# A layer out with the weights stationary and 384 tokens moving, its sums kept with outputs on partitions

## The chip, the core and the metric

The kernel runs on one core of a Trainium2 chip. The metric is the device time of one execution in microseconds (us), the median over several runs. The engines are named as in the profile: PE is the matrix engine (its weight loads stand apart as PEld), DVE is VectorE, ACT is ScalarE, POOL is GpSimd, and SP is the queue that issues nearly all DMAs. Each runs its own instructions in the order in which the program gives them.

## What is computed

Attention within chunks of 64 tokens, then a mixture of four experts with given shares (the first part), then a gated layer (the second part), in float32:

```python
attn = softmax(scale * q_c @ k_c.T); x = attn @ v_c        # (4, 8, 576, 64), 36 * 64 tokens a head
x = x.transpose(0, 2, 1, 3).reshape(2304, 512)
p = domain_probs / (domain_probs.sum(-1, keepdims=True) + 1e-09)
for e in range(4):
    out += p[:, e:e + 1] * (np.maximum(x @ w1[e], 0) @ w2[e])   # w1[e]: 512 x 1024, w2[e]: 1024 x 512
g = out @ w_gate; result = (g * sigmoid(g) * (out @ w_val)) @ w_out  # 1536 wide
```

## The kernel before, in words

The 2304 tokens go in three passes of 768 (six blocks of 128, or two halves of 384, `TT`). Part one runs over the passes, and in each over 16 sets of 256 hidden units, `sets`; two sets make a group (eight groups a pass, 24 in all, two groups to an expert). Part two does the same over the gated layer.

**Layer in** (`product`, lines 628 to 648; `half_k`, 618): a set's layer in is a 2x2 block product that is made of seven products, six matmuls each, weights stationary and 384 tokens moving. Each number is held as a rounded high part and a low part, and hi*hi, hi*lo and lo*hi are summed, three matmuls a term. The products' sums are put together by DVE (`plus`, 612) and kept by ACT (`keep`, 608). `done` (554) makes of a sum the hidden tile of a set: ACT writes the high part `hh` (559), DVE the low part `hl` (560), both [128 hidden units, 384 tokens].

**Layer out of part one** (`layer2`, 664 to 681): for each block of 128 tokens, four pieces of 128 hidden units with three matmuls each: the hidden tile's 128 tokens are stationary, 512 outputs of `w2` move, so a tile `y` in PSUM has tokens on partitions and is full after 12 matmuls. `gather` (751 to 764) multiplies it by the token's share `prob` of this expert, one number a partition, and adds it to the block's sum `acc`, in one DVE operation (762; 760 for the first group of a pass). After the last group of a pass `turn_x1` (768 to 777) turns each block's sum with four PE transposes, ACT copies it back, and SP stores it, since the next layer needs features on partitions.

**The order** is written out by hand (`order`, 1013 to 1020, and the loop from 1037). After every four and every three products there is a gap, in which the layer out of the group before gets its share of matmuls from the generator `two`: 18 where a group has two sets (1055), 12 for the first group (1044), 9 in each of the four steps `ahead` before the loop (993). `later` (162) puts a piece of work off by so many products. Weights for a product are made or loaded six products ahead (`LEAD`, `prepare`, 1026). `run_tasks` (966) lets background work in, among it the conversion of the second part's weights to its operands (`make_ops`, 452).

**Attention** of the first six blocks comes at the beginning, with the first products beside it; that of the other twelve is the list `rest` (953 to 957), whose stages (`att_scores`, `att_turn`, `att_values`, `att_out`: lines 255, 294, 317, 336) are done one at a time, four in the steps `ahead` and then after five of every seven products (1088). Scores are reduced and shifted by DVE (276, 277), exponentiated by ACT (283), turned by PE (287), multiplied with the values by PE (323), divided by DVE (330) and turned back by PE.

**Places in PSUM.** A `y` tile has two banks (`psY`), and two more (`psA`) once attention is through (1093). Until then the attention stages take turns in `psA`.

Of the kernel before, what the change touches and what calls it, by code (L numbers as in the profile page):

```python
# [10 lines left out]
F32 = mybir.dt.float32  # L11
# [80 lines left out]
def attention_moe_gated(  # L92
# [21 lines left out]
    ident = const.tile([P, P], F32, name="ident")  # L114
    prob = const.tile([P, NS, NE], F32, name="prob")

    xs = [dram.tile([2, P, KD, TT], F32, name=f"x_{s}") for s in range(2 * NPASS)]

    xt_d = [dram.tile([4, P, 2, TT], F32, name=f"xt_{s}") for s in range(2 * NPASS)]
    w_d = [dram.tile([NPROD, P, 2, 2 * P], F32, name=f"w_{n}") for n in range(NPAIRS + 2 * NPAIRS2)]  # L120
    w2_d = [dram.tile([P, 2, DM], F32, name=f"w2_{c}") for c in range(4 * NG1)]
# [40 lines left out]
    def later(d, f):  # L162
        deferred.setdefault(now[0] + d, []).append(f)
# [376 lines left out]

    gates = {}
    val, out_op = {}, {}
# [11 lines left out]
    def done(n, c, t, src):  # L554
# [8 lines left out]
        elif m == 0:  # L563
            sg = gates[c, t] = sg_p.tile([P, TT], F32, tag="sg", name=f"sg_{n}_{c}_{t}")

# [98 lines left out]
    def layer2(G):  # L664

        for b in range(BLOCKS):
            pool, tag = y_places[b % len(y_places)]
            y = pool.tile([P, DM], F32, tag=tag, name=f"y_{G}_{b}")
            c = slice(b % HALF * P, (b % HALF + 1) * P)
            for j in range(4):  # L670
                hh, hl = hid[G, j, b // HALF]
                w = w2op[G, j]
                nc.tensor.matmul(y, hh[:, c], w[:, 0], start=(j == 0), stop=False)  # L673
                yield
                nc.tensor.matmul(y, hh[:, c], w[:, 1], start=False, stop=False)  # L675
                yield
                nc.tensor.matmul(y, hl[:, c], w[:, 0], start=False, stop=(j == 3))  # L677
                if j < 3:
                    yield
            gather(G, b, y)  # L680
            yield

# [67 lines left out]

    def gather(G, b, y):
        part, s, g = part_of(G)
        a = s * BLOCKS + b
        if g == 0:
            acc[b] = acc_p.tile([P, DM], F32, tag="acc", name=f"acc{part}_{a}")
        sum_ = acc[b]
        if part == 1:
# [8 lines left out]
    turned = [-9]  # L766

    def turn_x1(s, b, sum_):
        turned[0] = now[0]
        src = sum_.rearrange("p (h k) -> p h k", k=CH)  # L770
        ps = transpose(att_ps(f"x1t_{s}_{b}", (psA, "a")), src).rearrange("p h k -> p (h k)")


        nc.scalar.copy(sum_, ps)
        half, c = divmod(b, HALF)
        d = xs[NPASS + s][half, :, :, c * P : (c + 1) * P]
        later(1, lambda: nc.sync.dma_start(d, sum_.rearrange("p (k t) -> p k t", t=P)))


    with tc.manual_schedule():  # L780
        acc_p = ctx.enter_context(tc.tile_pool(name="acc", bufs=8))
        h_p = ctx.enter_context(tc.tile_pool(name="h", bufs=12))
# [37 lines left out]
        clear(nc.gpsimd, vbd[2])  # L820
        clear(nc.gpsimd, vbd[3])
        nc.gpsimd.dma_start(prob, probs)
        att_load(0)
# [31 lines left out]
        def shares():  # L855

            sm = t_p.tile([P, NS], F32, tag="sum", name="prob_sum", bufs=3)
            nc.vector.tensor_reduce(out=sm, in_=prob, op=ALU.add, axis=AX.X)
            nc.vector.tensor_scalar_add(sm, sm, EPS)
            nc.vector.reciprocal(sm, sm)  # L860
            nc.gpsimd.tensor_tensor(out=prob, in0=prob, in1=sm.unsqueeze(2).to_broadcast(prob.shape), op=ALU.mult)

# [74 lines left out]
        for j in range(HALF):  # L937
            first_split("t2", j)
        tick()
        next_plain()  # L940
# [96 lines left out]
        for o in order:  # L1037
            if o is None:
# [4 lines left out]
                if G == 0:  # L1043
                    for _ in range(12):
                        next(two)
# [14 lines left out]
            if o == (N1, 0):  # L1060
                assert not tasks and not running, (len(tasks), len(running))
                raw64_cm.close()
                sg_p = ctx.enter_context(tc.tile_pool(name="sg", bufs=6, side="right"))
                wow_p = ctx.enter_context(tc.tile_pool(name="wow", bufs=2, side="right"))
# [23 lines left out]
            if rest and now[0] % NPROD < 5:  # L1088
                stage, a = rest.pop(0)
                stage(a, (psA, "a"))  # L1090
                if not rest:
# [30 lines left out]
def _lay_out(q, k, v, moe_domain_probs, moe_w1, moe_w2, moe2_w_gate, moe2_w_val, moe2_w_out):  # L1122
# [22 lines left out]
    def quads64(w):  # L1145
# [8 lines left out]
        "vt": np.ascontiguousarray(vt),  # L1154
        "probs": np.ascontiguousarray(moe_domain_probs.reshape(NS, P, NE).transpose(1, 0, 2)),
        "w1": np.ascontiguousarray(np.concatenate([quads(moe_w1[e]) for e in range(NE)])),
# [19 lines left out]
```

## Time and profile before

| | |
|---|---|
| median of 3 runs | 1246.08 us (1244.86 to 1246.33) |
| the profiled execution | 1245.16 us, its span 1243.3 us |
| PE, PEld busy | 1226.5 us (99%), 1131.5 us (91%) |
| DVE busy | 794.0 us (64%) |
| ACT, POOL busy | 538.7 us (43%), 595.3 us (48%) |
| DMA | 359.94 MB, mean 289 GB/s |

The span goes from the first to the last instruction of the profiled execution; about 2 us lie around it. Engines overlap, so the busy times don't add up. A matmul's duration in the profile is longer than its distance to the next one, since matmuls are pipelined: a run of them is measured from start to start. "Idle before" is the time in which an engine had nothing running ahead of an instruction, and the name behind it is what ended that wait.

### The profile page before, as it was taken

The page shows a single profiled execution, that of the slowest core. Times are in us where ns is not written, and L with a number is a line of the kernel's source. Part 1 is how long each engine was busy: PE and PEld are TensorE (multiplying, and loading weights), DVE is VectorE, ACT ScalarE, POOL GpSimd, SP SyncE. Part 2 cuts the span into 40 slices and gives each one's busy share as a digit, 9 for nine tenths or more (in the row PEclk, how much of TensorE's full clock was granted, in tenths as well). Part 3 has the DMA queues.
Part 4 walks back from the last instruction along what each step waited for, and adds up shares of the span by engine and source line. Part 5 has one row for each costly group of instructions (what it writes and reads, how often), then busy time and mean ns, then how long its engine had stood idle before and what let it go on. Part 6 is the DMA issues. An engine that isn't in the chain of part 4 may idle for free.

```text
span 1243.3 us, 21100 instructions
## 1 busy us (share of the span) xinstructions
PE 1226.5 (99%) x7216; PEld 1131.5 (91%) x7216; DVE 794.0 (64%) x1352; ACT 538.7 (43%) x1192; POOL 595.3 (48%) x611
## 2 busy tenths in 40 slices
PE   7999999999999999999999999999999999999998
PEld 6888888899888999898889889999999999999998
DVE  6766666666636766765566666455667656685576
ACT  4554434345424454544354344334435344344331
POOL 5553434477517776846376867312333222233221
PEclk9999999999999999999999999999999999999999
DMA  9588886799797999897899999866888797788774
GB/s 224 168 273 281 277 271 222 252 323 337 277 354 263 361 325 352 310 380 277 285 368 331 347 395 311 290 226 233 292 322 296 262 312 261 250 312 295 277 234 153
DMA packets 179594, 359.94 MB, mean 289 GB/s; under 512 B 19216, under 2 KB 46352, under 8 KB 179488
## 3 DMA queue, kind: packets, MB, share of 16 engines
q1 hardware_dynamic: 178688, 357.25, 82.6%
q10 hardware_dynamic: 768, 1.31, 0.4%
q8 instruction: 58, 0.95, 0.3%
q14 instruction: 48, 0.39, 0.1%
q0 software_dynamic: 32, 0.04, 0.0%
HBM read 258.90 MB, written 99.61 MB: 288 GB/s over the span
## 4 chain that ended last, share of the span: by engine, by line
PE 81%; DMA 7%; DVE 3%; issue 3%; POOL 2%; ACT 2%; SPq 1%; POOLq 0%; DVEq 0%; ACTq 0%
PE y L673 9%; PE y L677 9%; PE y L675 9%; PE lx L624 8%; PE lx L626 7%; PE lx L625 7%; PE ox L739 5%; PE lz L624 4%; PE oz L739 4%; PE lz L626 4%; PE lz L625 4%; DMA w<-w 3%; PE lw L624 2%; PE lw L626 2%; PE lw L625 2%
## 5 line engine op out<-in xcount | busy, mean ns | idle before, releaser
L673 PE MATMUL y<-w,hh 128*128 128x512 f32 x576 | 228.1, 396 | 0.0
L677 PE MATMUL y<-w,hl 128*128 128x512 f32 x576 | 226.4, 393 | 0.0
L675 PE MATMUL y<-w,hh 128*128 128x512 f32 x576 | 225.6, 392 | 0.2 <-POOL w L126 0.2
L126 POOL TENSOR_TENSOR w<-raw,w 128x256 fp32r<-128x256 f32 (+1 forms) x156 | 143.5, 938 | 149.7 <-ACT w L125 131.9
L126 POOL TENSOR_TENSOR ol<-sg,oh 128x384 fp32r<-128x384 f32 x72 | 80.5, 1129 | 267.1 <-ACT oh L125 225.7
L559 ACT ACTIVATE hh<-sum_p 128x384 fp32r<-128x384 f32 x90 | 47.2, 525 | 221.0 <-DVE sum_p L612 221.0
L762 DVE SCALAR_TENSOR_TENSOR acc<-y,prob,acc 128x512 f32<-128x512 f32 x126 | 91.1, 743 | 65.3 <-PE y L677 65.1
L677 PEld LDWEIGHTS y<-w,hl 128*128 128x128 f32 x576 | 108.0, 188 | 24.1
L673 PEld LDWEIGHTS y<-w,hh 128*128 128x128 f32 x576 | 108.2, 188 | 21.4 <-issue 1.4
L675 PEld LDWEIGHTS y<-w,hh 128*128 128x128 f32 x576 | 108.2, 188 | 21.3 <-POOL w L126 0.7
L612 DVE TENSOR_TENSOR sum_p<-lx,p 128x384 f32<-128x384 f32 x81 | 44.9, 554 | 94.7 <-PE lx L626 93.4
L560 DVE SCALAR_TENSOR_TENSOR hl<-sum_p,hh 128x384 fp32r<-128x384 f32 x90 | 63.0, 700 | 62.4 <-ACT hh L559 62.4
L126 POOL TENSOR_TENSOR w_made<-raw,w_made 128x256 fp32r<-128x256 f32 x84 | 68.3, 822 | 66.3 <-ACT w_made L125 54.3
L125 ACT ACTIVATE w<-raw 128x256 fp32r<-128x256 f32 (+1 forms) x156 | 67.5, 454 | 5.4 <-DVE raw L396 3.2
L125 ACT ACTIVATE oh<-sg 128x384 fp32r<-128x384 f32 x72 | 36.5, 525 | 70.4 <-DVE sg L573 70.0
L608 ACT COPY u<-lx 128x384 f32<-128x384 f32 x81 | 38.6, 477 | 65.0 <-PE lx L626 64.9
L624 PE MATMUL lz<-t1h,w 128*128 128x384 f32 x162 | 55.3, 341 | 1.7 <-DMA w<-w 1.7
L624 PE MATMUL lz<-b22h,w 128*128 128x384 f32 x162 | 55.8, 344 | 1.1 <-ACT p L608 0.9
L624 PE MATMUL lw<-b21h,w 128*128 128x384 f32 x162 | 54.8, 339 | 0.7 <-DMA w<-w 0.7
L125 ACT ACTIVATE o<-sg 128x384 fp32r<-128x384 f32 x54 | 26.5, 520 | 66.8 <-DVE sg L129 66.8
L624 PE MATMUL lx<-t2h,w 128*128 128x384 f32 x162 | 55.0, 340 | 0.3 <-DMA w<-w 0.3
L626 PE MATMUL lx<-t3h,w 128*128 128x384 f32 x162 | 54.9, 339 | 0.0
(270 smaller groups left out, 3421.0 us busy)
## 6 DMA issues: line engine op xcount, KB each, us to landing
w<-w SPq DMA_DIRECT2D x567, 256.0 KB, 5.3
w<-w SPq DMA_DIRECT2D x96, 512.0 KB, 6.0
w<-w_made SPq DMA_DIRECT2D x84, 256.0 KB, 5.7
wo_t<-wo_t SPq DMA_DIRECT2D x36, 512.0 KB, 4.8
wo_b<-wo_b SPq DMA_DIRECT2D x27, 512.0 KB, 4.2
raw<-w SPq DMA_DIRECT2D x19, 512.0 KB, 4.3
raw<-w SPq DMA_DIRECT2D x32, 256.0 KB, 4.3
sums<-x SPq DMA_DIRECT2D x40, 192.0 KB, 5.4
```

Source lines behind the costliest of these rows:

```text
L125: nc.scalar.activation(h, src, AF.Copy)
L126: (lo or nc.vector).tensor_tensor(out=l, in0=src, in1=h.bitcast(F32), op=ALU.subtract)
L559: nc.scalar.activation(h, src, AF.Relu)
L560: nc.vector.scalar_tensor_tensor(out=l, in0=src, scalar=0.0, in1=h.bitcast(F32), op0=ALU.max, op1=ALU.subtract)
L624: nc.tensor.matmul(ps, w[:, 0, c], xh[:, k], start=f, stop=False, skip_group_check=True)
L625: nc.tensor.matmul(ps, w[:, 0, c], xl[:, k], start=False, stop=False, skip_group_check=True)
L626: nc.tensor.matmul(ps, w[:, 1, c], xh[:, k], start=False, stop=e, skip_group_check=True)
L673: nc.tensor.matmul(y, hh[:, c], w[:, 0], start=(j == 0), stop=False)
L675: nc.tensor.matmul(y, hh[:, c], w[:, 1], start=False, stop=False)
L677: nc.tensor.matmul(y, hl[:, c], w[:, 0], start=False, stop=(j == 3))
L739: nc.tensor.matmul(o, left[:, c], w[:, k, right], start=start and t % 2 == 0 and k == 0 and i == 0, stop=k == 1 and i == 2, skip_group_che ...
L762: nc.vector.scalar_tensor_tensor(out=sum_, in0=y, scalar=p, in1=sum_, op0=ALU.mult, op1=ALU.add)
```

## The change

The weights of the layer out become the stationary operand, 128 outputs at a time, and a half's 384 hidden columns move. A `y` tile then has 128 outputs on partitions and 384 tokens along the row, and is full after 12 matmuls as before; there are eight such tiles a group (two halves, four output pieces) in place of six blocks. The share of a token now varies along the row, so a row of 384 shares is loaded for each half and expert, the same on all partitions (`load_share`), from a small tensor in DRAM to which the turned shares are written at the beginning (`shares_turn`). `gather` multiplies the tile by that row and then adds it to the sum, in two operations. The sums already stand with features on partitions, so `turn_x1` and its transposes go, and each sum is stored as it is. A tile buffer of attention goes (`e`, three to two), the stages in `rest` are put into another order, and two of the six places for sigmoid tiles move to another pool. At the beginning two weight splits come ahead of a block's softmax, and a background task starts three products later. Shares are laid out by expert on the host.

```diff
@@ layer2
-        for b in range(BLOCKS):
-            y = pool.tile([P, DM], F32, tag=tag, name=f"y_{G}_{b}")
-            c = slice(b % HALF * P, (b % HALF + 1) * P)
-            for j in range(4):
-                hh, hl = hid[G, j, b // HALF]
-                w = w2op[G, j]
-                nc.tensor.matmul(y, hh[:, c], w[:, 0], start=(j == 0), stop=False)
-                nc.tensor.matmul(y, hh[:, c], w[:, 1], start=False, stop=False)
-                nc.tensor.matmul(y, hl[:, c], w[:, 0], start=False, stop=(j == 3))
-            gather(G, b, y)
+        for half in range(2):
+            for k in range(KD):
+                y = pool.tile([P, DM], F32, tag=tag, name=f"y_{G}_{half}_{k}")[:, :TT]
+                c = slice(k * P, (k + 1) * P)
+                for j in range(4):
+                    hh, hl = hid[G, j, half]
+                    w = w2op[G, j]
+                    nc.tensor.matmul(y, w[:, 0, c], hh, start=(j == 0), stop=False)
+                    nc.tensor.matmul(y, w[:, 1, c], hh, start=False, stop=False)
+                    nc.tensor.matmul(y, w[:, 0, c], hl, start=False, stop=(j == 3))
+                gather(G, half, k, y)
@@ gather, turn_x1
-            p = prob[:, a, g * NE // NG1 : g * NE // NG1 + 1]
-            if g == 0:
-                nc.vector.tensor_scalar(out=sum_, in0=y, scalar1=p, scalar2=None, op0=ALU.mult)
-            else:
-                nc.vector.scalar_tensor_tensor(out=sum_, in0=y, scalar=p, in1=sum_, op0=ALU.mult, op1=ALU.add)
-            if g == NG1 - 1:
-                later(2 + b % 2, lambda: turn_x1(s, b, sum_))
-    def turn_x1(s, b, sum_):
-        ...
+    def load_share(s, e, half):
+        t = share[half] = pb_p.tile([P, TT], F32, tag=f"pb{half}", name=f"share_{s}_{e}_{half}")
+        a = e * NS + s * BLOCKS + half * HALF
+        row = p_d[a : a + HALF].rearrange("a t -> (a t)")
+        nc.sync.dma_start(t, row.unsqueeze(0).to_broadcast([P, TT]))
+        ...
+        nc.vector.tensor_tensor(out=sum_ if g == 0 else y, in0=y, in1=share[half], op=ALU.mult)
+        if g > 0:
+            nc.vector.tensor_tensor(out=sum_, in0=y, in1=sum_, op=ALU.add)
+        if k == KD - 1 and (g + 1) * NE // NG1 != e and (s, e) != (NPASS - 1, NE - 1):
+            later(2, lambda: load_share(*divmod(s * NE + e + 1, NE), half))
+        if g == NG1 - 1:
+            later(2, lambda: nc.sync.dma_start(xs[NPASS + s][half, :, k], sum_))
@@ the beginning
+        def shares_turn():
+            ps = att_ps("shares", where()).rearrange("p h k -> p (h k)")[: NE * NS, :P]
+            nc.tensor.transpose(ps, prob.rearrange("p e a -> p (e a)"), ident)
+            t = t_p.tile([P, P], F32, tag="sum", name="prob_turned", bufs=3)
+            nc.scalar.copy(t[: NE * NS], ps)
+            nc.sync.dma_start(p_d[:], t[: NE * NS])
         att_turn(3, where())
+        w_plain(0, ORDER[:2])
         att_soft(4)
         att_sums(3)
         att_exp(4)
-        w_plain(0, ORDER[:2])
         ...
         att_out(4, where())
+        shares_turn()
         att_values(5, where())
@@ order of attention, shares of the gaps, tasks
-        for a in range(BLOCKS, NS + 2):
-            for stage, b in ((att_scores, a), (att_values, a - 2), (att_turn, a - 1), (att_out, a - 2)):
+        for a in range(BLOCKS, NS + 1):
+            for stage, b in ((att_turn, a - 1), (att_scores, a), (att_values, a - 1), (att_out, a - 1)):
-            for _ in range(9):
+            for _ in range(12):
-                    for _ in range(12):
+                    for _ in range(16):
-                    for _ in range(12 * BLOCKS // (2 * size)):
+                    for _ in range(48 // size):
-            if o == (NPAIRS + 2, 1):
+            if o == (NPAIRS + 2, 4):
-            if not (last_of_pass(n) or last_of_pass(n + 1) and i >= 5 or now[0] - turned[0] < 2):
+            if not (last_of_pass(n) or last_of_pass(n + 1) and i >= 5):
@@ places
-        pool, how = (acc_p, dict(tag="acc")) if a < BLOCKS else (at_p, dict(tag="e", bufs=3))
+        pool, how = (acc_p, dict(tag="acc")) if a < BLOCKS else (at_p, dict(tag="e", bufs=2))
-            sg = gates[c, t] = sg_p.tile([P, TT], F32, tag="sg", name=f"sg_{n}_{c}_{t}")
+            pool, tag = (sg_p, "sg") if sg_count[0] % 6 < 4 else (raw2_p, "raw2")
+            sg_count[0] += 1
+            sg = gates[c, t] = pool.tile([P, TT], F32, tag=tag, name=f"sg_{n}_{c}_{t}")
```

## Rows read from the trace of the kernel before

**Rows 1.** The page, part 1: busy us, share of the span, instructions of each engine
```profile
PE 1226.5 (99%) x7216; PEld 1131.5 (91%) x7216; DVE 794.0 (64%) x1352; ACT 538.7 (43%) x1192; POOL 595.3 (48%) x611
```
**Rows 2.** Waits of PE, longest in total first: us, times, longest us
```profile
PE plz L624 <- ACT w L125: 2.3, 2, 1.9
```
**Rows 3.** Groups of DVE by form: count, busy us, mean ns of one, idle before
```profile
L762 DVE SCALAR_TENSOR_TENSOR acc<-y,prob,acc 128x512 f32<-128x512 f32 x126 | 91.1, 743 | 65.3 <-PE y L677 65.1
L560 DVE SCALAR_TENSOR_TENSOR hl<-sum_p,hh 128x384 fp32r<-128x384 f32 x90 | 63.0, 700 | 62.4 <-ACT hh L559 62.4
...
L612 DVE TENSOR_TENSOR sum_p<-lx,p 128x384 f32<-128x384 f32 x81 | 44.9, 554 | 94.7 <-PE lx L626 93.4 <-ACT raw L440 1.3
```
**Rows 4.** Waits of DVE from 450 to 500 us
```profile
DVE sum_p L612 <- PE lx L626: 5.1, 3, 1.8
DVE acc L762 <- PE y L677: 1.6, 1, 1.6
```
**Rows 5.** Waits of DVE from 500 to 550 us
```profile
DVE sum_p L612 <- PE lx L626: 2.3, 2, 1.7
```
**Rows 6.** Timeline of PE from 503 us: start us, duration us, instruction
```profile
504.07 0.39 PE L673 MATMUL y<-w,hh 128*128 128x512 f32 x1
...
508.24 0.34 PE L624 MATMUL lx<-t3h,w 128*128 128x384 f32 x1
...
512.43 0.39 PE L673 MATMUL y<-w,hh 128*128 128x512 f32 x1
...
519.72 0.39 PE L673 MATMUL y<-w,hh 128*128 128x512 f32 x1
```
**Rows 7.** Timeline of PE from 334 us, at a turn of a sum
```profile
334.59 0.60 PE L287 MATMUL x1t<-ident,acc 128*128 128x128 f32 x4
334.95 0.42 PE L624 MATMUL lz<-b22h,w 128*128 128x384 f32 x1
335.21 0.34 PE L625 MATMUL lz<-b22l,w 128*128 128x384 f32 x1
```
**Rows 8.** Timeline from 130 us: a block's values, their division, the next stage
```profile
131.92 1.09 PE L323 MATMUL av<-vbd,et 128*64 128x128 f32 x16
...
134.11 0.60 PE L287 MATMUL et<-ident,e 128*128 128x128 f32 x4
...
134.79 0.68 DVE L330 TENSOR_TENSOR e<-av,rs 128x512 f32<-128x512 f32 x1
```
**Rows 9.** Timeline from 55 us: raw sums, the first rest block's scores, its exponential
```profile
56.24 1.35 DVE L396 TENSOR_TENSOR raw<-raw 128x256 f32<-128x256 f32 x2
...
57.22 1.09 PE L261 MATMUL s<-kbd,q 128*64 128x128 f32 x16
...
59.81 0.63 ACT L283 ACTIVATE e<-e 128x512 f32<-128x512 f32 x1 [3.77 <-DVE e L277]
```
**Rows 10.** Timeline from 312 us: start of a group's layer out
```profile
312.37 0.39 PE L673 MATMUL y<-w,hh 128*128 128x512 f32 x1
...
314.41 0.54 DVE L560 SCALAR_TENSOR_TENSOR hl<-lx,hh 128x384 fp32r<-128x384 f32 x1
...
315.07 0.50 PE L675 MATMUL y<-w,hh 128*128 128x512 f32 x1 [0.22 <-POOL w L126]
```
**Rows 11.** Timeline from 535 us: start of a later group's layer out
```profile
535.56 0.39 PE L673 MATMUL y<-w,hh 128*128 128x512 f32 x1
...
537.28 0.54 DVE L560 SCALAR_TENSOR_TENSOR hl<-lx,hh 128x384 fp32r<-128x384 f32 x1
```
**Rows 12.** Timeline from 21 us
```profile
24.63 0.44 PE L624 MATMUL plz<-b11h,w 128*128 128x384 f32 x1 [1.91 <-ACT w L125]
```
**Rows 13.** Timeline from 34 us
```profile
35.65 1.09 PE L323 MATMUL av<-vbd,et 128*64 128x128 f32 x16
35.66 0.32 POOL L861 TENSOR_TENSOR prob<-prob,prob_sum 128x72 f32<-128x72 f32 x1
```
**Rows 14.** DMA issues: size, median us from issue to landing
```profile
sums<-x SPq DMA_DIRECT2D x40, 192.0 KB, 5.4
```

More of the change, by code (lines that the diff above doesn't have):

```diff
@@ L114, in attention_moe_gated @@
     ident = const.tile([P, P], F32, name="ident")
-    prob = const.tile([P, NS, NE], F32, name="prob")
     xs = [dram.tile([2, P, KD, TT], F32, name=f"x_{s}") for s in range(2 * NPASS)]
     xt_d = [dram.tile([4, P, 2, TT], F32, name=f"xt_{s}") for s in range(2 * NPASS)]
+    p_d = dram.tile([NE * NS, P], F32, name="p")
     w_d = [dram.tile([NPROD, P, 2, 2 * P], F32, name=f"w_{n}") for n in range(NPAIRS + 2 * NPAIRS2)]
@@ L539, in hidden_tiles @@
         return h, l
-    gates = {}
+    gates, sg_count = {}, [0]
     val, out_op = {}, {}
@@ L664, in layer2 @@
     def layer2(G):
[L666 to L681 removed]
+        for half in range(2):
+            for k in range(KD):
+                pool, tag = y_places[(half * KD + k) % len(y_places)]
+                y = pool.tile([P, DM], F32, tag=tag, name=f"y_{G}_{half}_{k}")[:, :TT]
[4 more added lines that the diff above has]
+                    nc.tensor.matmul(y, w[:, 0, c], hh, start=(j == 0), stop=False)
+                    yield
+                    nc.tensor.matmul(y, w[:, 1, c], hh, start=False, stop=False)
+                    yield
+                    nc.tensor.matmul(y, w[:, 0, c], hl, start=False, stop=(j == 3))
+                    if j < 3:
+                        yield
+                gather(G, half, k, y)
+                yield
     def layer_out(G):
@@ L749, in layer_out, with gather @@
                         yield
-    def gather(G, b, y):
-        part, s, g = part_of(G)
-        a = s * BLOCKS + b
-        if g == 0:
-            acc[b] = acc_p.tile([P, DM], F32, tag="acc", name=f"acc{part}_{a}")
-        sum_ = acc[b]
-        if part == 1:
-            p = prob[:, a, g * NE // NG1 : g * NE // NG1 + 1]
-            if g == 0:
-                nc.vector.tensor_scalar(out=sum_, in0=y, scalar1=p, scalar2=None, op0=ALU.mult)
-            else:
-                nc.vector.scalar_tensor_tensor(out=sum_, in0=y, scalar=p, in1=sum_, op0=ALU.mult, op1=ALU.add)
-            if g == NG1 - 1:
-                later(2 + b % 2, lambda: turn_x1(s, b, sum_))
-    turned = [-9]
-    def turn_x1(s, b, sum_):
[L769 to L777, printed above, removed]
+    share = {}
+    def load_share(s, e, half):
[3 more added lines that the diff above has]
+        nc.sync.dma_start(t, row.unsqueeze(0).to_broadcast([P, TT]))
+    def gather(G, half, k, y):
+        _, s, g = part_of(G)
+        e = g * NE // NG1
+        if g == 0:
+            acc[half, k] = acc_p.tile([P, DM], F32, tag="acc", name=f"acc1_{s}_{half}_{k}")[:, :TT]
+        sum_ = acc[half, k]
+        nc.vector.tensor_tensor(out=sum_ if g == 0 else y, in0=y, in1=share[half], op=ALU.mult)
[5 more added lines that the diff above has]
+            later(2, lambda: nc.sync.dma_start(xs[NPASS + s][half, :, k], sum_))
     with tc.manual_schedule():
+        pb_p = ctx.enter_context(tc.tile_pool(name="pb", bufs=1))
         acc_p = ctx.enter_context(tc.tile_pool(name="acc", bufs=8))
@@ L821, in attention_moe_gated @@
         clear(nc.gpsimd, vbd[3])
+        prob = t_p.tile([P, NE, NS], F32, tag="sum", name="prob", bufs=3)
         nc.gpsimd.dma_start(prob, probs)
@@ L857, in shares @@
             sm = t_p.tile([P, NS], F32, tag="sum", name="prob_sum", bufs=3)
-            nc.vector.tensor_reduce(out=sm, in_=prob, op=ALU.add, axis=AX.X)
+            nc.vector.tensor_reduce(out=sm, in_=prob.rearrange("p e a -> p a e"), op=ALU.add, axis=AX.X)
             nc.vector.tensor_scalar_add(sm, sm, EPS)
             nc.vector.reciprocal(sm, sm)
-            nc.gpsimd.tensor_tensor(out=prob, in0=prob, in1=sm.unsqueeze(2).to_broadcast(prob.shape), op=ALU.mult)
+            nc.gpsimd.tensor_tensor(out=prob, in0=prob, in1=sm.unsqueeze(1).to_broadcast(prob.shape), op=ALU.mult)
+        def shares_turn():
[4 more added lines that the diff above has]
+            nc.sync.dma_start(p_d[:], t[: NE * NS])
         def turn(a):
@@ L938, in attention_moe_gated @@
             first_split("t2", j)
+        for half in range(2):
+            load_share(0, 0, half)
         tick()
@@ L1062, in attention_moe_gated @@
                 raw64_cm.close()
-                sg_p = ctx.enter_context(tc.tile_pool(name="sg", bufs=6, side="right"))
+                sg_p = ctx.enter_context(tc.tile_pool(name="sg", bufs=4, side="right"))
                 wow_p = ctx.enter_context(tc.tile_pool(name="wow", bufs=2, side="right"))
@@ L1154, in _lay_out @@
         "vt": np.ascontiguousarray(vt),
-        "probs": np.ascontiguousarray(moe_domain_probs.reshape(NS, P, NE).transpose(1, 0, 2)),
+        "probs": np.ascontiguousarray(moe_domain_probs.reshape(NS, P, NE).transpose(1, 2, 0)),
         "w1": np.ascontiguousarray(np.concatenate([quads(moe_w1[e]) for e in range(NE)])),
```

## The prediction

> **What bounds the kernel now.** I read the busy shares first, then who PE waits for, then where VectorE (DVE) has room. PE is busy for 1226.5 of 1243.3 us [rows 1]; a busy PE alone proves little, so the waits come next: sixteen kinds, the largest 2.3 us, which lies in the first 30 us [rows 2]. So the sum is that of PE's stream: what leaves it is gained in full, and whatever makes PE wait is lost in full. DVE is busy for 64% [rows 1], but its free time isn't all room. It runs its work in order, and after each layer-in sum it stands idle until ScalarE has made the rounded half: 62.4 us before one of the three groups of such halves alone [rows 3]. What it could give away is the idle time that PE ends. That is 5.1 + 1.6 = 6.7 us of 50 at 450 to 500 [rows 4] and 2.3 us of 50 at 500 to 550 [rows 5]. The reader is to see a full PE beside an engine with little slack in just the part of the kernel that the change loads.
>
> **The stream itself.** A group's layer out is 72 matmuls of 512 moving columns before and 96 of 384 after: the same columns, a third more instructions. What 384 columns cost is shown by the layer-in products, which have that shape. In one stretch 18 y matmuls start at 504.07 and the next product at 508.24: 4.17 us. The 24 product matmuls behind them take 508.24 to 512.43: 4.19 us [rows 6]. So a gap's share (18 before, 24 after) costs 0.02 us more; 24 groups have 96 such shares: +1.9 us. Bounds: nothing if the rates are equal per column, and +5 us if each share costs 0.05 us more, some products being slower than these. I take 1.9, the rows being of the same shape and the same moment. The Trainium skill (TensorE: Matmul & The Clock Gate, section Back-to-back issue gap) gives a warm matmul N/2.4 + 2.5 ns; as an estimate from it, 576 more matmuls would cost 1.4 us, half a microsecond less than my term. The same section's sustained figures, 131 ns at 512 columns and 81 at 128, speak against the change: on a line between them 384 columns take 114 ns, and the estimate is 36 us slower. The trace has 232 ns where that page has 131, so here the measurement decides and that rule gets no chance.
>
> **The turned sums.** 18 blocks (six in each of three passes) lose four transposes each. One such turn starts at 334.59, the product behind it at 334.95, and that product's first matmul holds the next one back to 335.21: 0.36 + 0.26 us [rows 7], where a matmul of this shape alone takes 4.19 / 24 = 0.175. 0.36 + 0.26 - 0.18 = 0.44 us each; 18 of them: **-7.9 us**. PE had no idle time there that could have hidden them. ScalarE loses 18 copies of the turned sums; its share isn't on the path, so I count nothing. The six 256 KB stores of a pass become eight of 192 KB with the same bytes.
>
> **VectorE.** A y tile was one operation of 743 ns; it is now a multiplication that writes back into PSUM and an addition. No row shows DVE writing PSUM. The nearest is a 128x384 operation with one operand in PSUM, 554 ns; I have no reason to go lower, and the upper end is 700 ns, the mean of the 128x384 that contends for SBUF [rows 3]. I take 554, so 1.11 us per tile (0.55 in the first group of a pass, which only multiplies). A set of products (15.65 us, 504.07 to 519.72 [rows 6]) has three tiles before and four after: 4 x 1.11 - 3 x 0.74 = +2.2 us of DVE per set. At 450 to 500 there are 6.7 / 50 x 15.65 = 2.1 us of room per set, just enough; at 500 to 550 there are 0.7, too little [rows 4, 5]. So DVE runs late in places, and the question is what PE needs from it soon.
>
> First, the low half of the group's last hidden tile. Its subtraction stands in DVE's queue behind the gap's two tiles, which now take 2.22 instead of 1.49 us: 0.73 us later where DVE is behind already. It is needed by the twelfth y matmul of the next gap, which starts 11 x 0.174 = 1.92 us after the gap's first, not 11 x 0.232 = 2.55. At 312.37 the gap starts, and the subtraction ends at 314.95; 315.68 against 314.29 would be a wait of 1.4, of which 0.4 is there already (the eleventh matmul, which waits for POOL, starts at 315.07, where 312.37 + 10 x 0.232 = 314.69) [rows 10]: +1.0. At 535.56 and 537.82 [rows 11]: 538.55 against 537.48: +1.1. Elsewhere I see more room, though late tiles of the gap before may add as much again. I take +2.1, bounds 0 and +5.
>
> Second, attention, moved in its order. Before, a block's values and its last transposes had another block's turn between them; now there is one product. Where the block falls one product behind a gap, the values start at 131.92, DVE's division (queued behind the rest of the slot) ends at 135.47, and the stage that would now be those transposes starts at 134.11 [rows 8]: PE waits 1.4 us. By the list's order against the five slots of seven this happens to two blocks: +2.8. Three more come one slot later; with a product more, some 1.1 us, in between, 0.3 each: +0.9. The rest have a gap of 4.2 us in between: nothing. Bounds: 0 if the division overtakes nothing but comes sooner, +7 if DVE's added load delays all five by another 0.7.
>
> Third, in the first steps the first rest block is turned one step after its scores, not two. Scores at 57.22, exponential ended at 60.44 [rows 9]. Now the first y tile's multiplication (0.55) stands ahead of the two raw sums (1.35) that had been done by then, so the exponential ends some 0.9 us later, about 61.4, and the y matmuls in between end at about 60.4: +1.0, bounds 0 and 2.
>
> **The beginning.** Two weight splits go ahead of an exponential; the matmul at 24.63 waited 1.91 us for them [rows 12], so up to 1.9 is to be had. The turn of the shares is one transpose, which needs the divided shares; these end at 35.98 where PE would come at 35.65 [rows 13]: a wait of 0.3, and about 0.4 for itself. I take 0 for both, bounds -1.9 and +1.
>
> **Transfers.** 24 rows of shares are loaded, 192 KB each in SBUF; the nearest row of that size lands in 5.4 us [rows 14], and a row is needed two gaps or more after its load: nothing. Its issue on SP's queue waits for DVE's last tile of the half, and the weight loads queue behind it; they are issued six products ahead. The stores that waited there for a turned sum go. If a share row came late, each of 22 would cost up to a few us; I see no reason. The sigmoid tiles still come from six places, so they cost nothing.
>
> **Sum.** -7.9 + 1.9 + 2.1 + 2.8 + 0.9 + 1.0 + 0 = +0.8 us on the profiled execution's 1245.2, so 1246.0. The median of the runs shown is 0.9 us above that execution: **1247 us**. About 0.2%, 2.5 us, is what a measurement here can tell from no change; this is inside.
>
> **Rivals.**
> Faster, because the waits don't come: DVE takes its work earlier in gaps that now have two tiles evenly, and the late operations still have their few hundred ns. Then -7.9 + 1.9 = -6.0, 1240 us. For it: PE waits for DVE almost nowhere now [rows 2]. Against it: the transposes right behind their division [rows 8]. With half of the waits it is 1243.5. Chance 0.27.
> Slower, because DVE becomes the bound in pass two: it decides once a drain costs more than the room. If the addition takes 700 ns [rows 3], a tile takes 1.25 and a set 4 x 1.25 - 2.23 = 2.8 us more; at 500 to 550, 3.2 sets lack 2.1 each, at 450 to 500 0.7 each: 8.9 us, of which 1.1 stands in the sum already: 1247 + 8 = 1255. For it: the little room at 500 to 550 [rows 5]. Against it: the PSUM row of 554 [rows 3]. Chance 0.25.
> Slower through the instruction count: at the +5 bound of the stream, 1250. Chance 0.10.
>
> **Numbers.** The forecast has 0.38, with a range of its own from 1244 to 1249. Faster 0.27, same 0.38, slower 0.35. The range from 1240 to 1256 reaches to both rivals and leaves out the far sides, where all bounds fall together.
>
> **What would show it.** Right: no x1t rows; 24 y matmuls in 4.17 to 4.20 us; DVE busy up by some 90 us; PE rows that wait for "DVE e L330" at two blocks in the first 230 us and for the low half at a few group starts, 4 to 7 us in all. Wrong: PE waits under 2 us (first rival), DVE idle time ended by PE gone over tens of microseconds and PE waits over 12 us (second), y runs over 4.22 us (third), or waits of PE or DVE on a share row.

## The result and the profile after

The kernel after takes 1263.7 us (median of 6 runs, 1259.75 to 1267.34), the kernel before 1246.2 us beside it: a ratio of 1.0137 [1.0116, 1.0159], 17.5 us slower. The prediction was 1247 us with a range from 1240 to 1256, and the measured time lies 7.7 us beyond that range. The profiled execution after took 1264.46 us, its span 1262.7, 19.4 more than before. Of these, 18.5 us lie ahead of part two, whose first layer-out matmul starts at 868.7 us before and at 887.2 after.

Part 1 of the page, which answers to [rows 1]:

```profile
PE 1231.6 (98%) x7721; PEld 1204.7 (95%) x7721; DVE 882.8 (70%) x1568; ACT 529.6 (42%) x1175; POOL 595.7 (47%) x611
```

DVE is busy for 88.8 us more. The groups of DVE by form (as [rows 3]) show where they come from:

```profile
L768 DVE TENSOR_TENSOR y<-y,share 128x384 f32<-128x384 f32 x168 | 94.1, 560 | 71.6 <-PE y L680 70.8 <-DMA xt<-sums 0.6
L770 DVE TENSOR_TENSOR acc<-y,acc 128x384 f32<-128x384 f32 x168 | 93.7, 558 | 5.8
...
L614 DVE TENSOR_TENSOR sum_p<-lx,p 128x384 f32<-128x384 f32 x81 | 44.9, 554 | 28.1 <-PE lx L628 27.9 <-issue 0.2
```

A tile now takes two operations of 0.56 us, as priced. The idle time of DVE before this group of `sum_p` was 94.7 us in [rows 3] and is 28.1 now: in most cases DVE no longer waits for the product, but comes late to it. From 450 to 500 us its list of waits has no PE in it any more, where [rows 4] had 6.7 us:

```profile
DVE hl L560 <- ACT hh L559: 6.6, 9, 1.9
DVE neg L442 <- ACT neg L437: 2.2, 2, 2.0
```

From 500 to 550 us, where [rows 5] had 2.3 us, a wait for PE is still there, now ahead of the drain:

```profile
DVE y L768 <- PE y L680: 3.4, 5, 1.0
```

Over 400 to 760 us the idle time of DVE that PE ends falls from 63.8 to 20.7 us.

The waits of PE (us, times, longest) from 60 to 900 us, where the kernel before has three rows, of 0.2, 0.3 and 0.7 us:

```profile
PE xt L287 <- DVE e L330: 4.0, 5, 1.1
PE y L680 <- DVE hl L560: 3.6, 2, 2.0
PE lx L626 <- DMA w<-w: 3.4, 3, 2.1
PE lz L626 <- DVE hl L560: 1.9, 1, 1.9
PE y L678 <- POOL w L126: 1.5, 1, 1.5
PE lw L626 <- DMA w<-w: 1.0, 2, 0.5
PE lz L626 <- DMA w<-w: 0.7, 1, 0.7
```

These are 16.1 us in all: 9.5 behind DVE (attention's transposes and the low halves of hidden tiles), 1.5 behind POOL, and, not foreseen, 5.1 for weights that land late. One wait for a low half, in the timeline of DVE and then of PE (start, duration):

```profile
512.98 1.11 DVE L443 SCALAR_TENSOR_TENSOR top_wo<-top_wo,neg_wo 128x512 int32<-128x512 int32 x1
514.13 0.43 DVE L446 TENSOR_SCALAR neg_wo<-top_wo 128x512 int32<-128x512 int32 x1
514.47 0.56 DVE L768 TENSOR_TENSOR y<-y,share 128x384 f32<-128x384 f32 x1
515.06 0.56 DVE L770 TENSOR_TENSOR acc<-y,acc 128x384 f32<-128x384 f32 x1
515.54 0.56 DVE L768 TENSOR_TENSOR y<-y,share 128x384 f32<-128x384 f32 x1
516.13 0.56 DVE L770 TENSOR_TENSOR acc<-y,acc 128x384 f32<-128x384 f32 x1
516.60 0.55 DVE L560 SCALAR_TENSOR_TENSOR hl<-lx,hh 128x384 fp32r<-128x384 f32 x1
...
517.20 0.45 PE L680 MATMUL y<-hl,w 128*128 128x384 f32 x1 [1.59 <-DVE hl L560]
```

The matmul before this one started at 515.27. The low half that it needs stands in DVE's queue behind two operations of the background conversion of weights and behind both tiles of the gap before, with no idle time between. And a late weight load, in the timeline of PE:

```profile
537.25 0.34 PE L628 MATMUL lz<-b22h,w 128*128 128x384 f32 x1
539.67 0.41 PE L626 MATMUL lx<-b11h,w 128*128 128x384 f32 x1 [2.08 <-DMA w<-w]
...
541.94 0.52 PE L626 MATMUL lw<-b21h,w 128*128 128x384 f32 x1
542.26 0.52 PE L627 MATMUL lw<-b21l,w 128*128 128x384 f32 x1
```

After the wait, from 540.8 on, the matmuls start 0.32 us apart instead of 0.174: for 3.4 us the granted clock is at the lower of its two levels. There are three such stretches, from 496.4, 540.8 and 653.4 us on, and the windows that hold them (us, PE, PEld, DVE, ACT, POOL busy, granted clock, DMA share, GB/s) have a mean clock of 0.97:

```profile
450.00:500.00 50.00, 47.66 (x264) 47.05 (x263) 40.14 (x67) 24.02 (x55) 35.24 (x37) 0.97 0.97 343
500.00:550.00 50.00, 46.32 (x255) 45.54 (x254) 38.43 (x62) 20.86 (x46) 32.61 (x34) 0.97 0.81 289
...
650.00:700.00 50.00, 48.14 (x267) 48.14 (x268) 37.75 (x64) 22.57 (x50) 33.43 (x36) 0.97 0.93 330
```

Summed over the trace from matmul start to matmul start, the slow stretches cost 4.6 us, and single distances of matmuls of 256 columns and more that are over 120 ns too long cost 16.5 us more than before. So the loss is waits of PE first and its clock second.

### The profile page after: what moved, and what is told of

It reads as the page before. It is cut to its first block, busy times and chain, and to the rows that moved or that the text cites. A ratio compares the mean times of both kernels' runs of the same rounds, so it can differ in the third digit from the quotient of the medians.

```text
span 1262.7 us, 22352 instructions
## 1 busy us (share of the span) xinstructions
PE 1231.6 (98%) x7721; PEld 1204.7 (95%) x7721; DVE 882.8 (70%) x1568; ACT 529.6 (42%) x1175; POOL 595.7 (47%) x611
## 4 chain that ended last, share of the span: by engine, by line
PE 61%; DVE 11%; DMA 11%; issue 6%; POOL 4%; ACT 3%; SPq 2%; POOLq 0%; DVEq 0%; ACTq 0%
PE y L680 6%; PE y L676 6%; PE y L678 6%; PE lx L626 6%; PE lx L628 6%; PE lx L627 6%; DMA w<-w 5%; PE ox L742 5%; PE oz L742 4%; PE lz L626 3%; PE lz L628 3%; PE lz L627 3%; POOL w L126 2%; PE lw L626 2%; PE lw L628 1%
## 5 line engine op out<-in xcount | busy, mean ns | idle before, releaser
L680 PE MATMUL y<-hl,w 128*128 128x384 f32 x768 | 259.3, 338 | 3.6 <-DVE hl L560 3.6
L678 PE MATMUL y<-hh,w 128*128 128x384 f32 x768 | 258.9, 337 | 1.5 <-POOL w L126 1.5
L676 PE MATMUL y<-hh,w 128*128 128x384 f32 x768 | 260.3, 339 | 0.0
L680 PEld LDWEIGHTS y<-hl,w 128*128 128x128 f32 x768 | 145.1, 189 | 4.5 <-DVE hl L560 4.5
L678 PEld LDWEIGHTS y<-hh,w 128*128 128x128 f32 x768 | 145.2, 189 | 2.3 <-POOL w L126 2.1
L676 PEld LDWEIGHTS y<-hh,w 128*128 128x128 f32 x768 | 145.1, 189 | 1.5 <-issue 1.2
L768 DVE TENSOR_TENSOR y<-y,share 128x384 f32<-128x384 f32 x168 | 94.1, 560 | 71.6 <-PE y L680 70.8
L560 DVE SCALAR_TENSOR_TENSOR hl<-sum_p,hh 128x384 fp32r<-128x384 f32 x90 | 57.6, 640 | 63.0 <-ACT hh L559 63.0
L770 DVE TENSOR_TENSOR acc<-y,acc 128x384 f32<-128x384 f32 x168 | 93.7, 558 | 5.8
L614 DVE TENSOR_TENSOR sum_p<-lx,p 128x384 f32<-128x384 f32 x81 | 44.9, 554 | 28.1 <-PE lx L628 27.9
L626 PE MATMUL lx<-b11h,w 128*128 128x384 f32 x162 | 54.7, 338 | 3.6 <-DMA w<-w 3.4
L614 DVE TENSOR_TENSOR sum_p<-lw,p 128x384 f32<-128x384 f32 x81 | 44.7, 552 | 18.4 <-PE lw L628 15.6
```

Of the source, the lines that this page charges most:

```text
L614: nc.vector.tensor_tensor(out=t, in0=ps, in1=snap.pop(name), op=ALU.add)
L626: nc.tensor.matmul(ps, w[:, 0, c], xh[:, k], start=f, stop=False, skip_group_check=True)
L676: nc.tensor.matmul(y, w[:, 0, c], hh, start=(j == 0), stop=False)
L678: nc.tensor.matmul(y, w[:, 1, c], hh, start=False, stop=False)
L680: nc.tensor.matmul(y, w[:, 0, c], hl, start=False, stop=(j == 3))
L768: nc.vector.tensor_tensor(out=sum_ if g == 0 else y, in0=y, in1=share[half], op=ALU.mult)
```

## The experiments

There are four suspects: DVE's second operation, attention's order, the queue of the loads, and the stream itself. Each experiment ran beside the kernel before (1245.8 to 1246.4 us); the kernel after was not run again, so "after" is 1263.7 us throughout. Traces are of one execution of each kernel. Diffs are shortened.

**The second operation, put into the kernel before.**
```diff
-    nc.vector.scalar_tensor_tensor(out=sum_, in0=y, scalar=p, in1=sum_, op0=ALU.mult, op1=ALU.add)
+    nc.vector.tensor_scalar(out=y, in0=y, scalar1=p, scalar2=None, op0=ALU.mult)
+    nc.vector.tensor_tensor(out=sum_, in0=y, in1=sum_, op=ALU.add)
```


> The kernel before with its drain in two operations instead of one: the tile is multiplied by the share in PSUM and then added, both 128x512. Everything else is as before. DVE gains some 80 to 90 us. Theory 1: the same waits as in the kernel after show up in pass two, 1255 us or more (12 to 17 us above before, less what the larger room between three tiles a set hides). Theories 2 and 3: 1246 to 1248 us.


Measured: 1254.92 us, +9.1 (ratio 1.0067 [1.0054, 1.008]). DVE's busy time rose from 794.0 to 871.2 us, and PE's waits have the row that the kernel before hasn't:

```profile
PE y L677 <- DVE hl L560: 2.8, 2, 2.4
PE xt L287 <- DVE e L330: 0.9, 2, 0.5
```

That is just under what the first theory asked for, and far above the others: DVE's load alone makes the kernel before slower, with the old operand order. The wait for the low half is back in this trace, and 3.4 us at the lower clock follow it; waits for weights stay small (0.8 us from 60 to 900 us).

**The second operation, taken out of the kernel after.**
```diff
-    nc.vector.tensor_tensor(out=sum_ if g == 0 else y, in0=y, in1=share[half], op=ALU.mult)
+    if g == 0:
+        nc.vector.tensor_copy(out=sum_, in_=y)
```


> The kernel after without the multiplication by the share row: a tile is only added to the sum (the first group of a pass copies it), so DVE has one operation of about 0.56 us a tile instead of two, and falls from 883 to some 790 us busy. The share rows are still loaded, with no reader. Theory 1 (DVE's second operation makes it late in pass two, and PE's waits for the low halves, the late weight loads and the clock drops follow from that): the stalls beyond attention's (12 us) and the slow stretches (4.6 us) go, 1247 us (1244 to 1251). Theory 2 (the share rows and the stores of the sums block the queue of the weight loads): the loads and stores still go out, 1258 or more. Theory 3 (the stream of 96 shorter matmuls and attention's order cost it, in PE's own stream): 1258 or more.


Measured: 1255.8 us, 7.9 less than after. No theory had that: the second operation is worth a little under half of the loss. In the traces, whose spans differ by 11.0 us, the three stretches at the lower clock are gone (4.6 us), and the waits of PE from 60 to 900 us fall from 16.1 to 9.9. What stays is led by:

```profile
PE lx L626 <- DMA w<-w: 3.2, 3, 1.8
PE xt L287 <- DVE e L330: 2.7, 5, 0.8
PE y L680 <- DVE hl L560: 2.5, 2, 2.1
```

The waits for weights are nearly all still there (3.6 us of 5.1), so they don't come from the second operation alone.

**The order of attention, put into the kernel before.**
```diff
-    for a in range(BLOCKS, NS + 2):
-        for stage, b in ((att_scores, a), (att_values, a - 2), (att_turn, a - 1), (att_out, a - 2)):
+    for a in range(BLOCKS, NS + 1):
+        for stage, b in ((att_turn, a - 1), (att_scores, a), (att_values, a - 1), (att_out, a - 1)):
```


> The kernel before with the list of the rest of attention in the order of the kernel after, and nothing else. If the order alone makes the five waits of the transposes for the division (4.7 us net in the trace after): 1250.5 us. If these waits are DVE's second operation ahead of the division: 1247 to 1248.5 us, with two waits of about 1 us.


Measured: 1250.84 us, +5.0 (ratio 1.0034 [1.0021, 1.0047]). The order alone does it, with DVE's drains as short as before (743 ns):

```profile
PE xt L287 <- DVE e L330: 2.3, 4, 0.8
```

The row lists only idle time. From the matmul before to the first transpose the four took 1.10, 0.64, 1.10 and 0.88 us, and a fifth 0.44, where a matmul takes 0.17: 3.3 us lost in all.

**The order of attention, put back in the kernel after** (the diff above reversed, and places for a third `e` tile):
```diff
-    e ... bufs=2        # and sum tiles bufs=3
+    e ... bufs=3        # and sum tiles bufs=2
-    part = st_p.tile([P, H, w], F32, tag="hs", name=f"hs{a}", bufs=1)
+    part = pb_p.tile([P, TT], F32, tag="pb0", ...)
-    prob = t_p.tile([P, NE, NS], F32, tag="sum", name="prob", bufs=3)
+    prob = const.tile([P, NE, NS], F32, name="prob")
```


> The kernel after with the list of the rest of attention in the order of the kernel before and three e tiles; room for them comes from two sum tiles instead of three and from one small tile kept elsewhere. If the order is worth as much as in the kernel before (+5.0 us there): 1258 to 1259.5 us, with no wait of the transposes for the division. If the third sum tile was needed, waits of DVE for ACT's high half, and less gain. The spacing of the layer-out matmuls of part two, 120 ns after against 117.5 before, shows whether where the tiles lie plays a part in it.


Measured: 1253.6 us, 10.1 less than after, twice the expected. The transposes wait no more for the division, and the layer-out matmuls of part two are back at 117.3 ns, which is 2.3 us and belongs to the places of tiles, not to the order. The other waits stayed, so the order was a term of its own:

```profile
PE y L680 <- DVE hl L560: 4.6, 3, 3.0
PE lx L626 <- DVE top L435: 2.3, 1, 2.3
PE lx L626 <- DMA w<-w: 1.8, 3, 1.2
```

**Where the tiles lie.** Both kernels with one unused tile of 32 bytes ahead of all others:
```diff
     ident = const.tile([P, P], F32, name="ident")
+    pad = const.tile([P, 8], F32, name="pad")
+    nc.vector.memset(pad, 0.0)
```


> The kernel after with one unused tile of 32 bytes a partition ahead of all others, so that every tile behind it lies 32 bytes further on; nothing else changes but one memset at the beginning. If it is the place of the operands in SBUF that makes the layer-out matmuls of part two 120 ns apart in the kernel after and 117.5 before: 117.5 here, 2.3 us less there and perhaps 0.9 in the y runs, 1260 to 1262 us. If it is not: 120 ns, 1263 to 1265.

> The same tile of 32 bytes in the kernel before. If the place plays a part: the layer-out matmuls of part two go from 117.5 to 120 ns apart, 1248 to 1250 us. If it is not: 1245 to 1247.5.


Measured: 1260.2 us (1256.37 to 1264.15), 3.5 less than after, though the runs of the two overlap, and 1246.58 us, no change (ratio 1.0002). Layer out of part two in the timeline of PE, first in the kernel after, then with the shift; the same 15 matmuls lie between the two rows of each:

```profile
1008.38 0.40 PE L742 MATMUL oz<-wo_b,oh 128*128 128x256 f32 x2
...
1010.18 0.40 PE L742 MATMUL oz<-wo_b,oh 128*128 128x256 f32 x2
```

```profile
1001.85 0.39 PE L744 MATMUL oz<-wo_b,oh 128*128 128x256 f32 x2
...
1003.61 0.40 PE L744 MATMUL oz<-wo_b,oh 128*128 128x256 f32 x2
```

These are 1.80 and 1.76 us: 120 ns apart against 117.3, in code that the change did not touch. Over the 1133 matmuls of that layer out it is some 2.9 us. The place counts, but which place is slow these runs don't settle: the constants, ahead of most other tiles, take 512 bytes a partition in the kernel after, and 544 (this one), 800 (before, and order back) or 832 (before, shifted) elsewhere. All five traces with 512 show 120 ns, the twelve others 117 to 118.

**The turns.** The kernel before stores its sums unturned, and keeps the pause of two products that the background work makes behind each turn:
```diff
-    ps = transpose(att_ps(f"x1t_{s}_{b}", (psA, "a")), src).rearrange("p h k -> p (h k)")
-    nc.scalar.copy(sum_, ps)
```


> The kernel before without the four transposes and the copy of each turned sum: the sum is stored as it stands, with tokens on partitions. It prices the removal alone. By the forecast's row 18 turns of 0.44 us: 1238 us (1236.5 to 1239.5). If the turns filled time in which PE would wait for something else (the rival), 1242 or more, with new waits of PE at the ends of the passes.


Measured: 1242.21 us, -4.2 (ratio 0.9969 [0.9958, 0.998]), about half of the forecast. The transposes' own distances, 6.4 us of PE, are gone, but the products, which have the matmuls behind them, lost nothing in sum (606.9 us before, 607.0 here): a late load took back what they gained. The loads' row, 0.3 us before:

```profile
PE lx L624 <- DMA w<-w: 1.9, 2, 1.7
```

In the two traces 6.2 us are gone from the first layer-in product `lx` on (69.4 us before, 70.8 here). Ahead of it, where the edit changes nothing, this trace is 1.3 us later and has 3.4 us at the lower clock at 24.6 us. So by these two readings the turns are worth 4.2 to 6.2 us.

**The share rows' queue.** All shares loaded once:
```diff
-    if k == KD - 1 and (g + 1) * NE // NG1 != e and (s, e) != (NPASS - 1, NE - 1):
-        later(2, lambda: load_share(*divmod(s * NE + e + 1, NE), half))
```


> The kernel after with the two share rows loaded once, at the beginning, and used for all experts and passes: 22 loads of 192 KB and their waits on SP's queue are left out, both DVE operations stay. Theory 1 (DVE's load): no change, 1262 to 1265 us. Theory 2 (these loads block the queue of the weight loads, and so make PE wait for weights): the waits of PE for weight loads (6 us above those of before) and the clock drop behind one of them (1.5 us) go, 1256 or less.


Measured: 1263.67 us, as after. The repeated share loads cost nothing.

**The place of the low halves.** In a group's first two tiles, what needs the last low half comes last (the order of matmuls in short, not the code's lines):
```diff
-    for k in range(KD): for j in range(4): hh*w0, hh*w1, hl*w0
+    for k in (0, 1): for j in range(4): hh*w0 (and hh*w1, hl*w0 for j < 3)
+    for k in (0, 1): hh*w1, hl*w0 for j = 3, then gather
```


> The kernel after with the matmuls of a group's first two y tiles in another order: those that need the low half of the last hidden tile, or the low half of the last weights, come last, at the end of the gap, and both tiles are drained there. The operations of all engines stay the same. If it is the place of that low half (the twelfth matmul, 1.9 us after the gap's start) that turns DVE's lateness into waits, the two waits for it (3.9 us), the wait for the weights' low half (1.5) and the clock drops behind them (3 us) go: 1255 to 1257 us. If DVE is simply the bound, its lateness only comes out at the next product or tile: 1261 or more.


Measured: 1260.86 us (1259.65 to 1262.84), 2.8 less, with runs that overlap those of after: nearer to "it only comes out elsewhere". The wait for the low half fell from 3.6 to 0.5 us and others rose. Both tiles are now drained at the gap's end; that this is what makes a division and the conversion late is argued, not shown:

```profile
PE xt L287 <- DVE e L330: 6.4, 7, 1.7
PE lx L626 <- DVE top L435: 2.9, 1, 2.9
```

**The background work.** Thinner in pass two, denser in pass three:
```diff
-    run_tasks(2)
+    run_tasks(1 if n < 2 * NPAIRS and now[0] % 2 else 3 - (n < 2 * NPAIRS))
```


> The kernel after with the background work thinned in pass two (one step after every second product, two after the others, instead of two after each) and three steps in pass three. If the second operation hurts because pass two is crowded by the conversion of the second part's weights (DVE 80% busy, the DMA queues over 90%), the waits for low halves and for weight loads between 450 and 720 us shrink by half, with at least one of the clock drops: 1256 to 1259 us. If the crowd is no part of it: 1262 to 1265, and a move of waits to pass three.


Measured: 1279.33 us, 15.6 more than after. The windows (columns as above), first after, then thinned:

```profile
400.00:560.00 160.00, 153.86 (x858) 151.93 (x857) 125.54 (x203) 74.06 (x165) 113.02 (x121) 0.98 0.92 326
560.00:720.00 160.00, 155.49 (x878) 153.63 (x877) 118.69 (x192) 73.20 (x159) 110.92 (x110) 0.99 0.94 338
720.00:880.00 160.00, 159.92 (x916) 159.05 (x916) 104.08 (x181) 58.03 (x122) 59.12 (x60) 1.00 0.81 286
```

```profile
400.00:560.00 160.00, 158.60 (x912) 158.28 (x911) 116.36 (x197) 66.86 (x146) 81.44 (x88) 1.00 0.86 306
560.00:720.00 160.00, 148.15 (x803) 144.38 (x802) 125.68 (x187) 73.61 (x165) 130.61 (x128) 0.96 0.93 338
720.00:880.00 160.00, 153.54 (x859) 151.26 (x858) 106.25 (x179) 60.09 (x129) 70.19 (x72) 0.98 0.80 280
```

Where DVE and POOL got 9 and 32 us less to do, PE gained 4.7 us of busy time and the clock stayed up; where the work came later, PE lost 7.3 and 6.4 and the clock fell. So the crowd is the condition, as the theory said, but the expected gain was wrong: later stretches have no more room.

**The start of the background work**, moved by the change from product 1 to product 4 of a set; put alone into the kernel before, and moved back to product 1, one set later, on top of best_a below:
```diff
-    if o == (NPAIRS + 2, 1):
+    if o == (NPAIRS + 2, 4):     # before_tasks_4; best_a_phase has (NPAIRS + 3, 1)
```


> The kernel before with the background tasks started at product 4 of the set instead of product 1, as the kernel after does it; nothing else. The late weight loads at starts of sets (near 430, 450, 530, 613 and 700 us) are in the traces of the kernel after and of all its variants, with one operation a tile too, and not in the kernel before with two. If they come from where in a set the conversion's steps, loads and stores fall: these waits show up here, 4 to 6 us in all, 1250 to 1252 us. If they come from the layer out itself: no change, 1245.5 to 1247.5.

> As best_a, with the background tasks started at product 1 of the next set, the place within a set that the kernel before has, one set later. If the place within a set makes the weight loads late: the waits for them (6 us in best_a between 430 and 720 us) and the clock drop behind the longest go, 1244 to 1247 us. If not: 1250 to 1253, or more where the work that is now later crowds pass three.


Measured: 1248.98 us, +3.1 (ratio 1.0019 [1.0008, 1.003]), and 1254.96 us, 3.5 above best_a. In the first trace one load is late, and 3.4 us at the lower clock follow it:

```profile
PE lx L624 <- DMA w<-w: 3.1, 1, 3.1
```

So the start costs some 3 us in the kernel before, less than expected, and in the one trace kept it does so by a late load near 370 us. In the kernel after that load is hardly late: the matmul there starts 0.6 us after the one before it (at 372.9 us), so this term isn't seen in its trace. That the place within a set makes the later loads late (430 to 720 us) is not borne out by the second run, which starts a whole set later as well. What makes those late stays open. In the timeline of SP ahead of the wait at 537, the load of raw weights waits for POOL, 7.6 us, and then ten transfers are issued in 5.3 us, the late one among them:

```profile
522.62 0.38 SPq L412 DMA_DIRECT2D w<-w  x1
530.67 0.33 SPq L461 DMA_DIRECT2D raw<-wg  x1
...
534.87 0.61 SPq L412 DMA_DIRECT2D w<-w  x1
```

The loads of this line take 6.4 to 7.3 us to land there, 5.4 in the median of the kernel. But before has such stops of SP as well (up to 5.8 us at 440 to 460), and PE doesn't wait.

One candidate stands in no run. Before, the background work paused for two products behind each turn of a sum (`now[0] - turned[0] < 2`); the change drops that pause with the turns. Six of the turns fall between 574 and 606 us. The windows from 550 on, before and then after:

```profile
550.00:600.00 50.00, 49.98 (x257) 44.64 (x256) 30.58 (x43) 22.87 (x48) 25.23 (x21) 1.00 0.88 312
```

```profile
550.00:600.00 50.00, 50.00 (x289) 50.00 (x289) 38.68 (x60) 24.86 (x51) 31.93 (x28) 1.00 0.90 325
```

POOL has 6.7 us more to do there, and 3.8 us of PE's waits and one stretch at the lower clock follow between 618 and 657 us. That they follow from it is not shown.

**Do the parts add up?** The kernel after without the multiplication and with attention's order back (the edits of add_only and after_att_order_back together):


> The kernel after without the multiplication by the share row, and with the order of attention (and the places of tiles) of after_att_order_back: what is left of the change is the other operand order of the layer out, the missing turns and the tasks' start. If the parts add up: 1255.8 - 10.1 = 1245.7 us, that is 3.5 above the kernel before without its turns, as much as the clean spacing of the y runs costs (2304 x 174 ns against 1728 x 230 ns). If order and second operation overlap in what they make late, less is gained: 1248 or more.


Measured: 1247.76 us (1245.94 to 1252.02), 2.1 above the sum of the two gains, so the two overlap a little at most. What is left of the change stands 5.6 us above before_no_turn. The spacing of the y runs, the tasks' start and the dropped pause are in it; how it divides among them is not shown.

**Can it be saved?** Order back and low halves last, then with POOL taking every fourth addition in passes two and three:
```diff
+    there = s > 0 and 0 < g < NG1 - 1 and k == 2     # best_b only: product in SBUF, addition on POOL
+    (nc.gpsimd if there else nc.vector).tensor_tensor(out=sum_, in0=to, in1=sum_, op=ALU.add)
```


> The kernel after with both edits that helped: the rest of attention in the order of before, and the low halves of a group's first two y tiles last. If the gains add up (10.1 and 2.8 us): 1250 to 1252 us. If the order of attention and the late low halves were the same lateness of DVE counted twice: 1253 or more. DVE's second operation stays, so the late weight loads and a clock drop behind one of them stay.

> As best_a, and in passes two and three (but for their first and last groups) one tile in four is multiplied into SBUF and added to its sum by POOL: DVE loses 0.56 us a set there and POOL gains about 1.1. If DVE's load in pass two is what is left: 1247 to 1250 us. If POOL, busy for 70% there, is late instead (it makes the low halves of the converted weights, for which the next raw weights wait in SP's queue): no better than best_a, with longer waits for weight loads.


Measured: 1251.5 us (ratio 1.0034 [1.0022, 1.0046]) and 1253.91 us. The time of best_a is what the two gains give when added (1250.8), with the smaller one inside the spread of the runs. In best_b the waits for low halves at the layer out are gone (1.9 us in best_a) and those for weights are longer (the row of `lx`, 2.1 us in best_a), as the second theory had it. That POOL is the next engine without room fits (busy 188.6 us of 450 to 700, 174.6 in best_a), but is not shown:

```profile
PE lx L626 <- DMA w<-w: 6.1, 4, 3.4
```

Neither version beats the kernel before.

## Why the prediction was wrong

The terms, each by its own run or trace: turns -4.2, y spacing +3.9, second operation +7.9, order of attention +5.0, start of the tasks +3.1, place of the tiles +2.4 (the layer out of part two, 135.4 us before and 137.8 after). Sum +18.1, measured +17.5. That the sum comes so close is luck in good part. The order was worth 10.1 in the kernel after, places of tiles included; the tasks' start was priced by a late load that the kernel after hardly has; the dropped pause has no price; and by its runs the place of the tiles is not clear of the spread.

- **The turned sums, -7.9: mis-sized**, by the runs -4.2. Their 6.4 us on PE went. The 0.08 us by which the matmul behind a turn is longer (0.26 less 0.18, [rows 7]; 1.5 us for all 18) was taken back by a late load.
- **The stream, +1.9: too small.** Over all undisturbed distances a 512-column matmul takes 229.9 ns, one of 384 takes 174.1: 96 x (24 x 0.1741 - 18 x 0.2299) = +3.9. The 4.17 us that I took for a share of 18 [rows 6] was a slow one; the mean is 4.14. The Trainium skill (TensorE: Matmul & The Clock Gate, section Back-to-back issue gap) gives N/2.4 + 2.5 ns for a warm matmul; as an estimate from it, 384 columns take 162.5 ns and 512 take 215.8. The traces don't agree: both distances are longer, and the 1.4 us estimated from it was too small as well.
- **VectorE's price: right** (560 and 558 ns for 554, 88.8 us for some 90). **What PE pays for it, +2.1: this step failed.** I set the extra 2.2 us a set against the idle time that PE ends, called 2.1 at 450 to 500 "just enough", and then looked for the late low half at two group starts, each 0.73 us later. But room on average is not room at the moment: conversion steps stand in the same queue (the rows at 513 to 517), so the low half came 1.6 us late for PE there, and a stretch at the lower clock followed some of these waits. It cost 7.9 us, 9.1 in the kernel before. My bound of 5 was too low. The second rival (DVE becomes the bound, 1255, chance 0.25) named the mechanism and its signs came: two thirds of DVE's idle time that PE ended is gone between 400 and 760 us, and PE's waits are over 12 us. Even it held neither a lower clock nor the late weights. The weights are no part of this term, since they are late with one operation a tile too (3.6 us).
- **Attention, +2.8 +0.9 +1.0 = 4.7: right in sum** (5.0), partly by luck. Five blocks wait, as said. Less a matmul's own 0.17 us, two of them wait 1.24 us and the other three 0.49 to 1.15 rather than 0.3, 4.8 in all; the first rest block, priced at 1.0, waits not at all.
- **The beginning, 0: about right.** The first `lx` product starts at 68.65 us, 0.8 sooner than before.
- **Transfers, 0: right** for the share rows (shares_once); the late weight loads, 5.1 us of waits, were in no term. **The start of the tasks** I named and did not cost: 3.1 us in the kernel before. The dropped pause I did not see.
- **The place of the tiles** was in no term.

## What to carry to other kernels

When an engine gets a second operation in a place where it has "just enough" room, ask what else stands in its queue just ahead of the operation that PE needs next, and double that engine's operation in the old kernel: one run here gave 9.1 us as the price, which reading had given as 2. When one change holds five edits, price each alone in the kernel before; three of these cost 3 to 9 us each. A gain from removed PE work is safe only as far as its operands still come in time when PE gets there sooner.

## What had not been expected of the hardware

- Three waits of PE, with 2.2 to 2.4 us from one matmul's start to the next (at 493.0, 537.3 and 649.5 us), were each followed by 3.4 us at the lower clock, 1.2 GHz. The length of a wait alone doesn't decide it: the kernel after with the shift has a distance of 2.9 us (at 513.0 us), add_only one of 2.4 (at 640.2), and neither was followed by a lower clock. The runs of the kernel after spread with the clock: 1259.75 us at a mean granted clock of 0.999, 1267.34 at 0.995.
- 32 bytes of shift changed the spacing of matmuls in untouched code from 120 to 117.3 ns.
- DVE writing its product back into PSUM (560 ns) costs about what writing to SBUF with one operand in PSUM does (554 to 558).
